# Two VectorE slots in score phases with three free banks when few PV matmuls are queued, and redrawn seeds

## Chip, cores, metric

One core of a Trainium2 chip. The metric is the device time of one execution in microseconds (us); medians of several runs are quoted.

## The reference, cut

Layer norm of `x` (2048 x 512, bf16), then multi-query attention with 32 heads of 16 and one shared K and V, times a gate from a two-layer SiLU network, plus the residual:

```python
xn = _layernorm(x)
s = _A_ref(xn, A_wq, A_wk, A_wv, A_wo)      # softmax(q k^T / 4) v, then wo; 32 heads, one K and V
g = _silu(_B_ref(xn, B_w1, B_w2))           # silu(silu(xn @ w1) @ w2), inner width 1792
return x + s * g
```

## The kernel before

The kernel contains a *planner*: a program that runs when the kernel is built, models the engines, and decides in what order every engine gets its instructions. The chip then follows that order, with semaphore waits where data need them. So a rule of the planner is no instruction; it changes only the order and the grouping.

What matters here:

- PE computes a *score phase*: three or four matmuls K x Q, each of 32 rows, into as many PSUM banks (`L860`, or `L859` in the changed file). One bank of scores is one *slot*.
- Each slot goes to ScalarE (an exact exp, `pa_sb`, then one PV matmul) or to VectorE (an approximation: one pass that writes bits, `db_sb`, and three shifted copies of these made by GpSimd integer adds, `ds_sb`, so four PV matmuls).
- Between phases PE works off *rounds* of four column-tiled matmuls: PV products from a queue (`L1228`, later `L1266`), or a *job*, a piece of the q, h, z or output projections (`L505`, later `L510`). A running job holds one of the seven banks.

How the planner splits the banks of a phase, before:

```python
n = len(banks)                     # banks free for this phase, at most 4
ab = act_need() - t                # how far ahead ScalarE is supplied
...
else:                              # three or four banks
    want = 2 if n == 4 or ab > a_low else 1      # slots for VectorE
...
want = min(want, 2 if bl < two else 1 if bl < one else 0)   # bl: VectorE's backlog
```

Thresholds such as `a_low`, `two`, `one` are shaken by seeded noise, and the seed is replaced every 64 phases:

```python
SEEDS, STRETCH, SPREAD = (1020, 3123, 1104, 3421, 7220, 2660, 1802, 97), 64, 0.1
def vary(x):
    return x * (1.0 + SPREAD * (rng[-1].random() - 0.5)) if rng else x
```

The softmax here doesn't subtract the row's maximum and nothing guards it: scores larger than these inputs give would overflow.

## Time and profile before

| | before |
|---|---|
| median of the runs | 672.18 us (672.05 to 672.34, 4 runs) |
| span of the profiled run | 670.41 us |
| start to first score phase | 11.04 us |
| floor of 632 cycles (worked out in the prediction) | 624.35 us |
| waits in these cycles | 9.40 us |
| nine other gaps (prologue) | 14.66 us |
| last score phase to end | 10.97 us |

The three parts of the middle and the two ends add up to the span (to 0.01 us). A *cycle* is the time from the start of one score phase to the start of the next, where only rounds lie between; its floor is what the steady beat of the trace gives (0.435 us for the phase, 0.2165 for each round; a count, not a measurement), and what exceeds the floor is called a wait. The profile's lines for this are shown in the prediction.

### The profile page before, as it was taken

The numbers are of one execution on the slowest core, as the hardware profiler recorded it, in microseconds if no ns is written. First come the engines' busy times: TensorE is split into PE (matmuls) and PEld (weight loads), VectorE is DVE, ScalarE is ACT, GpSimd is POOL, SyncE is SP. The second block draws the span as 40 slices with busy tenths as digits, with TensorE's granted clock in tenths as the row PEclk, the third lists the DMA queues.
The fourth block names the chain that finished last, engine by engine and source line by source line (L and its number), as shares of the span: only waits on it lengthen the run. The fifth ranks groups of instructions, "written<-read, shape, count | busy, mean of one in ns | idle before, by whom it ended". The sixth has DMA issues, their size and how long they took to land.

```text
span 670.4 us, 21190 instructions
## 1 busy us (share of the span) xinstructions
PE 658.4 (98%) x8958; PEld 191.4 (29%) x8958; DVE 608.6 (91%) x1085; ACT 651.5 (97%) x756; POOL 566.7 (85%) x564
## 2 busy tenths in 40 slices
PE   7999999999999999999999999999999999999997
PEld 4422222222222222222222222222222222222223
DVE  8989999999999999999899999998979999999963
ACT  6999999999999999999999999999999999999995
POOL 3049899998998889989899988898989998889993
PEclk9999999999999999999999999999999999999999
DMA  9500000000000000000000010000000000100000
GB/s 299 165 9 2 2 2 2 2 3 2 2 1 18 18 18 17 2 2 2 2 2 2 2 33 18 18 2 1 2 2 2 2 2 17 34 18 2 2 2 32
DMA packets 11821, 12.86 MB, mean 19 GB/s; under 512 B 1808, under 2 KB 11216, under 8 KB 11728
## 3 DMA queue, kind: packets, MB, share of 16 engines
q1 hardware_dynamic: 10928, 10.78, 5.0%
q8 instruction: 72, 1.18, 0.7%
q10 hardware_dynamic: 800, 0.72, 0.3%
q14 instruction: 21, 0.17, 0.1%
HBM read 8.95 MB, written 2.10 MB: 16 GB/s over the span
## 4 chain that ended last, share of the span: by engine, by line
PE 78%; ACT 12%; DVE 8%; issue 1%; DMA 0%; ACTq 0%; DVEq 0%
PE ps L1228 34%; PE ps L860 26%; PE ps L505 18%; ACT pa_sb L1572 11%; DVE db_sb L1090 3%; DVE stats_sb L452 1%; ACT t_sb L652 1%; DVE u_sb L654 1%; DMA ds_sb<-in_A_x_dram 0%; DVE xnT_sb L532 0%; DVE xn_sb L481 0%; DVE fin_sb L712 0%; DVE f_sb L1275 0%; DVE mv_sb L456 0%; DVE kt_sb L561 0%
## 5 line engine op out<-in xcount | busy, mean ns | idle before, releaser
L1157 POOL INT64_ADD ds_sb<-db_sb x552 | 561.0, 1038 | 87.5 <-DVE db_sb L1090 33.2
L1572 ACT ACTIVATE pa_sb<-ps 128x1024 bf16<-128x1024 f32 (+2 forms) x667 | 619.0, 1040 | 6.4 <-PE ps L860 3.5
L1090 DVE TENSOR_SCALAR db_sb<-ps 128x512 uint16<-128x512 f32 x736 | 474.4, 682 | 38.8 <-PE ps L860 27.5
L1228 PE MATMUL ps<-ds_sb,v_sb 128*32 128x512 bf16 x2208 | 265.9, 383 | 0.0
L860 PE MATMUL ps<-qt_sb,kt_sb 32*128 32x512 bf16 x2048 | 251.8, 385 | 4.4 <-ACT pa_sb L1572 1.1
L1228 PE MATMUL ps<-pa_sb,v_sb 128*32 128x512 bf16 x1312 | 242.4, 383 | 0.0
L1228 PE MATMUL ps<-db_sb,v_sb 128*32 128x512 bf16 x736 | 165.0, 384 | 0.3 <-DVE f_sb L1275 0.3
L860 PEld LDWEIGHTS ps<-qt_sb,kt_sb 32*128 32x128 bf16 x2048 | 63.1, 91 | 277.6 <-ACT pa_sb L1572 149.8
L1228 PEld LDWEIGHTS ps<-ds_sb,v_sb 128*32 128x32 bf16 x2208 | 65.6, 95 | 62.8 <-issue 46.1
L505 PE MATMUL ps<-xnT_sb,w_sb 128*32 128x512 bf16 x896 | 73.2, 384 | 0.0
L1228 PEld LDWEIGHTS ps<-pa_sb,v_sb 128*32 128x32 bf16 x1312 | 59.6, 95 | 36.5 <-issue 24.9
L505 PE MATMUL ps<-w_sb,u_sb 128*32 128x512 bf16 x816 | 64.2, 384 | 0.0
L1228 PEld LDWEIGHTS ps<-db_sb,v_sb 128*32 128x32 bf16 x736 | 40.9, 95 | 21.5 <-issue 14.5
L652 ACT ACTIVATE t_sb<-ps 128x512 bf16<-128x512 f32 x72 | 45.1, 627 | 0.0
L654 DVE SCALAR_TENSOR_TENSOR u_sb<-t_sb,ps 128x512 bf16<-128x512 bf16 x56 | 38.3, 683 | 1.3 <-ACT t_sb L652 0.3
L694 PE MATMUL ps<-w_sb,u_sb 32*128 32x512 bf16 x80 | 30.8, 385 | 0.0
L505 PEld LDWEIGHTS ps<-xnT_sb,w_sb 128*32 128x32 bf16 x896 | 17.5, 94 | 26.6 <-issue 20.6
L654 DVE SCALAR_TENSOR_TENSOR tmp_sb<-t_sb,ps 128x512 bf16<-128x512 bf16 x16 | 11.0, 688 | 12.3 <-ACT t_sb L652 12.2
L505 PEld LDWEIGHTS ps<-w_sb,u_sb 128*32 128x32 bf16 x816 | 15.6, 95 | 22.3 <-issue 18.5
L1275 DVE STREAM_TRANSPOSE f_sb<-ps 128x512 f32<-128x512 f32 x31 | 21.9, 707 | 0.1
L505 PE MATMUL ps<-wo_sb,on_sb 128*32 128x512 bf16 x256 | 19.2, 383 | 0.0
L505 PE MATMUL ps<-xnT_sb,wq_sb 128*32 128x512 bf16 x240 | 18.9, 384 | 0.0
(71 smaller groups left out, 161.9 us busy)
## 6 DMA issues: line engine op xcount, KB each, us to landing
w_sb<-in_B_w_dram SPq DMA_DIRECT2D x2, 1792.0 KB, 13.4
xr_sb<-in_A_x_dram SPq DMA_DIRECT2D x16, 128.0 KB, 2.3
out_dram<-ob_sb SPq DMA_DIRECT2D x16, 128.0 KB, 1.7
ds_sb<-in_A_x_dram SPq DMA_DIRECT2D x3, 512.0 KB, 6.9
wq_sb<-in_A_wq_dram SPq DMA_DIRECT2D x1, 512.0 KB, 5.1
wo_sb<-in_A_wo_dram SPq DMA_DIRECT2D x1, 512.0 KB, 16.0
kt_sb<-kt_sb ACTq DMA_DIRECT2D x4, 112.0 KB, 4.2
ds_sb<-in_A_x_dram ACTq DMA_DIRECT2D x2, 128.0 KB, 2.9
```

The lines of the kernel that those rows point to most:

```text
L452: ts_ = pl.add(Task(DV, 593.0, lambda v, t=t: v.bn_stats(stats_sb[:, t, :], x_tile(t)), [xkey(t)], [("st", t)], 1 + j, gate=(lambda j=j: S ...
L505: last = h.matmul(bank(b)[32 * j:32 * (j + 1), 0:n], lhsT=lhs(j), rhs=rhs, start=start, stop=stop, tile_position=(0, 32 * j), skip_group_c ...
L652: t1 = Task(AC, 490.0, lambda a: a.activation(t_sb[:, k, :], src, ACT.Tanh, scale=scale), [held], [("t", k)], 0, [t0])
L654: t2 = Task(DV, T_P, lambda v: v.scalar_tensor_tensor(out=dst, in0=t_sb[:, k, :], scalar=1.0, in1=src, op0=ALU.add, op1=ALU.mult), [held, ...
L694: return (lambda pe: pe.matmul(bank(b), lhsT=u_sb[rows, ft, r * P:(r + 1) * P], rhs=w2_sb[rows, ft, :], start=False, stop=last, tile_posit ...
L860: return pe.matmul(bank(b), lhsT=kt_sb[32 * i:32 * i + 32, g % 2, kt * P:(kt + 1) * P], rhs=qt_sb[32 * i:32 * i + 32, (g // 2) % NQR, :], ...
L1090: bt.P[i] = pl.add(Task(DV, T_P, lambda v, b=b, i=i, bb=bt.b: v.tensor_scalar(db_sb[:, bb, i * NQ:(i + 1) * NQ], bank(b), 128.0 * LOG2E, 1 ...
L1157: whole["po"].append(pl.add(Task(PO, T_P64, lambda g, cols=cols: g.int64_add(ds_sb[:, s, cols].bitcast(U64), db_sb[:, bt.b, cols].bitcast( ...
L1228: h = pe.matmul(bank(OB)[32 * i:32 * (i + 1), :], lhsT=lhs, rhs=rhs, start=s0, stop=s1, tile_position=(0, 32 * i), skip_group_check=True)
L1275: t1 = pl.add(Task(DV, T_TR, lambda v: v.transpose(f_sb[:, k, :], bank(OB)), [("ps", OB)], [("F", k)], 1, [norm.get(("m", g - 2))]))
L1572: op = pl.place(AC, 0.8333 * NQ * n + T_AF, lambda a: a.activation(pa_sb[:, s * NQ:(s + n) * NQ].rearrange("p (b n) -> p b n", n=NQ), ps3[ ...
```

## The change

The intent: a VectorE slot brings four PV matmuls, a ScalarE slot one. If PV work for the two open groups runs low, PE may go idle, so give VectorE more. The core of the diff:

```diff
-SEEDS, STRETCH, SPREAD = (1020, 3123, 1104, 3421, 7220, 2660, 1802, 97), 64, 0.1
-PIECE_MIN = 4
+SEEDS, STRETCH, SPREAD = (1020, 3123, 1104, 3421, 6268, 3265), 64, 0.2
+PIECE_MIN = {"z": 4, "h": 9, "q": 9, "w": 9}
...
+LATE, QUEUE = 0.0, 10
+Q3, Q4, J3, J4, N3, N4, SOLO = 10, -1, 1, 2, 1, 2, 0
...
-                want = 2 if n == 4 or ab > a_low else 1
...
+                queue = sum(len(q) for g in range(st["gO"], min(st["gO"] + 2, NG)) for q in pvq[g])
+                held = any(not a.fixed for a in active)
+                if held:
+                    want = J4 + (queue < vary(Q4)) if n == 4 else J3 + (queue < vary(Q3))
+                else:
+                    want = N4 if n == 4 else max(N3, 2 * (queue < vary(QUEUE)))
+                if ab > a_low:
+                    want = 2
```

Cut: a common helper that would let q, h and output jobs run row-tiled pieces (the limit of nine rounds is never reached), an extra slot in a bank that frees late, a filler for unfinished pieces (neither fires), switches that are off, and a condition on when the tail is made.

More of the change, by code (lines that the diff above doesn't have):

```diff
@@ L42 @@
 K = len(SHIFT)
+PH = []
 PE, AC, DV, PO, SP = "PE", "ACT", "DVE", "POOL", "SP"
@@ L65 @@
 EVAC = ()
-P3, AP3 = 0, 14
+LATE, QUEUE = 0.0, 10
+Q3, Q4, J3, J4, N3, N4, SOLO = 10, -1, 1, 2, 1, 2, 0
+END_DV = 0
+METER, RATE, R0 = (), 1.0, 1.0
 WIDE, NMIN, EARLY = 3, 3, 300.0
@@ L381, in bass_recurrent_scan__grouped_kv_mqa__dense_activation_silu__prompt_kernel @@
         outs = []
+        PH.clear()
         xv = xf.rearrange("(t p) d -> p t d", p=P)
@@ L497, in job @@
             jb.preds, jb.bank, jb.fixed, jb.mode, jb.gate = preds, bk, bk is not None, mode, gate
-            jb.pos, jb.end, jb.got, jb.left, jb.piece, jb.prev = 0, len(rounds), set(), len(rounds), None, None
+            jb.due, jb.pos, jb.end, jb.got, jb.left, jb.piece, jb.prev = None, 0, len(rounds), set(), len(rounds), None, None
             jb.tasks = {}
@@ L599, in xnT_ready, with product, rnd, mk @@
             return all(k in pl.lastw for k in xnT_keys(c))
+        def product(jb, lhs, rhs, needs):
+            n = len(jb.rounds)
+            def rnd(k):
+                def mk(b):
+                    last = jb.left == 1
+                    return lambda pe: col4(pe, b, lambda j: lhs(k, slice(0, P), 32 * j, 32), rhs(k, slice(0, P)), k == 0, last)
+                return mk
+            def piece(k, i, last):
+                rows, b = slice(32 * i, 32 * i + 32), jb.bank
+                return (lambda pe: pe.matmul(bank(b), lhsT=lhs(k, rows, 0, P), rhs=rhs(k, rows), start=False, stop=last,
+                                             tile_position=(32 * i, 0), skip_group_check=True), needs(k))
+            jb.rounds = [(rnd(k), needs(k), MM) for k in range(n)]
+            jb.piece = piece
         def mk_q(oi):
             c, o = divmod(oi, NOC)
-            def rnd(dc):
-                def mk(b):
-                    return lambda pe: col4(pe, b, lambda j: wq_sb[:, dc, P * o + 32 * j:P * o + 32 * (j + 1)],
-                                           xnT_sb[:, dc, c * NQ:(c + 1) * NQ], dc == 0, dc == NDC - 1)
-                return mk
             def consume(jb, op):
@@ L615, in consume @@
                 return [t]
-            job("q", oi, max(0.0, 2 * oi - Q_LEAD), [(rnd(dc), ["wq"] + xnT_keys(c), MM) for dc in range(NDC)],
-                consume,
-                gate=lambda: xnT_ready(c) and (oi < NQR or left_oct[oi - NQR] == 0))
+            jb = job("q", oi, max(0.0, 2 * oi - Q_LEAD), [None] * NDC, consume,
+                     gate=lambda: xnT_ready(c) and (oi < NQR or left_oct[oi - NQR] == 0))
+            product(jb, lambda k, rows, a, n: wq_sb[rows, k, P * o + a:P * o + a + n],
+                    lambda k, rows: xnT_sb[rows, k, c * NQ:(c + 1) * NQ], lambda k: ["wq"] + xnT_keys(c))
         def mk_q0(ta, tb, bk):
@@ L666, in mk_h @@
         def mk_h(c, ft, pace):
-            def rnd(dc):
-                def mk(b):
-                    return lambda pe: col4(pe, b, lambda j: w1_sb[:, dc, P * ft + 32 * j:P * ft + 32 * (j + 1)],
-                                           xnT_sb[:, dc, c * NQ:(c + 1) * NQ], dc == 0, dc == NDC - 1)
-                return mk
             def consume(jb, op):
@@ L678, in consume @@
                 return u_task[c, ft].first
-            job("h", (c, ft), pace, [(rnd(dc), ["w1"] + xnT_keys(c), MM) for dc in range(NDC)], consume)
+            jb = job("h", (c, ft), pace, [None] * NDC, consume)
+            product(jb, lambda k, rows, a, n: w1_sb[rows, k, P * ft + a:P * ft + a + n],
+                    lambda k, rows: xnT_sb[rows, k, c * NQ:(c + 1) * NQ], lambda k: ["w1"] + xnT_keys(c))
         def mk_z(tt, pace):
             c, r = divmod(tt, 4)
-            def rnd(ft):
-                def mk(b):
-                    last = jb.left == 1
-                    return lambda pe: col4(pe, b, lambda j: u_sb[:, ft, r * P + 32 * j:r * P + 32 * (j + 1)],
-                                           w2_sb[:, ft, :], ft == 0, last)
-                return mk
-            def piece(ft, i, last):
-                rows, b = slice(32 * i, 32 * i + 32), jb.bank
-                return (lambda pe: pe.matmul(bank(b), lhsT=u_sb[rows, ft, r * P:(r + 1) * P], rhs=w2_sb[rows, ft, :],
-                                             start=False, stop=last, tile_position=(32 * i, 0), skip_group_check=True),
-                        ["w2", ("u", ft)])
             def consume(jb, op):
@@ L703, in consume @@
                 return tmp_task[tt].first
-            jb = job("z", tt, pace, [(rnd(ft), ["w2", ("u", ft)], MM) for ft in range(NFT)], consume,
+            jb = job("z", tt, pace, [None] * NFT, consume,
                 gate=lambda: all((c, ft) in u_task and u_task[c, ft].op is not None for ft in range(NFT))
                 and (tt < 8 or tt - 8 in fin_task and fin_task[tt - 8].op is not None))
-            jb.piece = piece
+            product(jb, lambda k, rows, a, n: u_sb[rows, k, r * P + a:r * P + a + n],
+                    lambda k, rows: w2_sb[rows, k, :], lambda k: ["w2", ("u", k)])
         def scaled(tt, b):
@@ L736, in mk_w @@
             c, r = divmod(tt, 4)
-            def rnd(o):
-                def mk(b):
-                    return lambda pe: col4(pe, b, lambda j: on_sb[:, (NOC * c + o) % NON, r * P + 32 * j:r * P + 32 * (j + 1)],
-                                           wo_sb[:, o, :], o == 0, o == NOC - 1)
-                return mk
             def consume(jb, op):
@@ L749, in consume @@
                 return [t1]
-            job("w", tt, pace, [(rnd(o), ["wo", ("on", (NOC * c + o) % NON)], MM) for o in range(NOC)], consume,
-                gate=lambda: all(oi in t2_task and t2_task[oi].op is not None for oi in range(NOC * c, NOC * c + NOC))
+            jb = job("w", tt, pace, [None] * NOC, consume,
+                     gate=lambda: all(oi in t2_task and t2_task[oi].op is not None for oi in range(NOC * c, NOC * c + NOC))
                 and tmp_task.get(tt) is not None and tmp_task[tt].op is not None and tt in xr_task)
+            product(jb, lambda k, rows, a, n: on_sb[rows, (NOC * c + k) % NON, r * P + a:r * P + a + n],
+                    lambda k, rows: wo_sb[rows, k, :], lambda k: ["wo", ("on", (NOC * c + k) % NON)])
         mk_T([0], 0)
@@ L798, in bass_recurrent_scan__grouped_kv_mqa__dense_activation_silu__prompt_kernel @@
                 mk_w(sp[1], pace)
+        work = [jb for jb in jobs if jb.piece is not None and jb.kind in METER]
+        for j1, j2 in zip(work, work[1:]):
+            j1.due = j2.pace
         for tt in range(4):
@@ L970, in pe_start, with pick_d, pass_d, placed @@
             return max(t, last[-1].end + SWITCH)
+        def pick_d(avoid, t):
+            bt = d_batch()
+            if bt is None:
+                return None
+            need = [i for i in range(4) if i not in bt.slots and i not in avoid and left[bt.g, i] and slot_ok(bt.g, i)
+                    and slot_time(bt.g, i) <= t + 30]
+            if not need:
+                return None
+            i = max(need, key=lambda i: len(left[bt.g, i]))
+            avoid.add(i)
+            if not bt.slots:
+                batches.append(bt)
+                db_busy[bt.b] = 1
+            kt = take(bt.g, i)
+            bt.slots[i] = kt
+            return bt, bt.g, i, kt
+        def pass_d(b, bt, g, i, kt):
+            tot[g, i] += K
+            def placed(pop):
+                pool_free.append(b)
+                pvq[g][i].append((pop, v_lhs(1, g, kt), db_sb[:, bt.b, i * NQ:(i + 1) * NQ].bitcast(BF16),
+                                  [("Db", bt.b, i)] + v_reads(1, kt), ("d", bt)))
+            bt.P[i] = pl.add(Task(DV, T_P, lambda v: v.tensor_scalar(
+                db_sb[:, bt.b, i * NQ:(i + 1) * NQ], bank(b), 128.0 * LOG2E, 128.0 * (SHIFT_BETA + 127.0),
+                op0=ALU.mult, op1=ALU.add), [("ps", b)], [("Db", bt.b, i)], 0, on_place=placed))
         def do_S(t):
@@ L985, in do_S @@
             else:
-                want = 2 if n == 4 or ab > a_low else 1
-                tri = any(y - x == 2 for x, y in zip(sorted(banks), sorted(banks)[2:]))
-                if n == 4 and tri and (P3 == 1 or P3 == 2 and st.get("la", 2) == 2 or P3 == 3 and not [a for a in active if not a.fixed] or P3 == 4 and st.get("la", 2) == 2 and not [a for a in active if not a.fixed] or P3 == 5 and bl > 600 or P3 == 6 and a_pressure() >= AP3):
-                    want = 1
+                queue = sum(len(q) for g in range(st["gO"], min(st["gO"] + 2, NG)) for q in pvq[g])
[6 more added lines that the diff above has]
+                    want = 2
             pj = None
-            if n == 3 and pl.mode != "S":
+            late = [b for r, b in bank_times()[n:] if r <= t + LATE]
+            if bl > one or not want_d():
+                late = []
+            if n == 3 and pl.mode != "S" and not late:
                 for jb in active:
-                    if jb.piece is not None and jb.pos > 0 and (jb.got or jb.end - 1 - jb.pos >= PIECE_MIN):
+                    if jb.piece is not None and jb.pos > 0 and (jb.got or jb.end - 1 - jb.pos >= PIECE_MIN[jb.kind]):
                         pj = jb
@@ L999, in do_S @@
             while len(dslots) < want and want_d():
-                bt = d_batch()
-                if bt is None:
+                d = pick_d(avoid, t)
+                if d is None:
                     break
-                need = [i for i in range(4) if i not in bt.slots and i not in avoid and left[bt.g, i] and slot_ok(bt.g, i) and slot_time(bt.g, i) <= t + 30]
-                if not need:
-                    break
-                i = max(need, key=lambda i: len(left[bt.g, i]))
-                avoid.add(i)
-                if not bt.slots:
-                    batches.append(bt)
-                    db_busy[bt.b] = 1
-                kt = take(bt.g, i)
-                bt.slots[i] = kt
-                dslots.append((bt, bt.g, i, kt))
+                dslots.append(d)
             nd = len(dslots)
@@ L1034, in do_S @@
             abanks = best[1]
+            solo = False
+            if SOLO and len(sl) == 3:
+                pairs = [(x, y, z) for x in banks for y in banks for z in banks if z == y + 1 and x not in (y, z)]
+                if pairs:
+                    abanks, solo = min(pairs, key=lambda p: abs(p[0] - p[1])), True
             dbanks = [b for b in banks if b not in abanks]
@@ L1074, in do_S @@
             st["phases"] = st.get("phases", 0) + 1
+            PH.append((op.t0, any(not a.fixed for a in active), n, len(sl), nd, act_need() - op.t0 - MM, dve_backlog(), a_pressure(), sum(len(q) for g in range(st["gO"], min(st["gO"] + 2, NG)) for q in pvq[g])))
             if st["phases"] % STRETCH == 0 and len(SEEDS) > len(rng):
@@ L1078, in do_S @@
                 u = Unit()
-                u.slot, u.bank, u.vis = sl_, b, pl.vis(op, AC)
+                u.slot, u.bank, u.vis, u.solo = sl_, b, pl.vis(op, AC), solo and b == abanks[0]
                 units.append(u)
@@ L1082, in do_S @@
                 tot[g, i] += 1
-            for b, (bt, g, i, kt) in zip(dbanks, dslots):
-                tot[g, i] += K
-                def placed(pop, b=b, g=g, i=i, kt=kt, bt=bt):
-                    pool_free.append(b)
-                    pvq[g][i].append((pop, v_lhs(1, g, kt), db_sb[:, bt.b, i * NQ:(i + 1) * NQ].bitcast(BF16),
-                                      [("Db", bt.b, i)] + v_reads(1, kt), ("d", bt)))
-                bt.P[i] = pl.add(Task(DV, T_P, lambda v, b=b, i=i, bb=bt.b: v.tensor_scalar(
-                    db_sb[:, bb, i * NQ:(i + 1) * NQ], bank(b), 128.0 * LOG2E, 128.0 * (SHIFT_BETA + 127.0),
-                    op0=ALU.mult, op1=ALU.add), [("ps", b)], [("Db", bt.b, i)], 0, on_place=placed))
+            for b, d in zip(dbanks, dslots):
+                pass_d(b, *d)
+            late = [b for b in late if b in pool_free]
+            while late and len(seen) < 4 and len(dslots) < (2 if bl < two else 1) and want_d():
+                used = set(seen)
+                d = pick_d(used, t)
+                if d is None:
+                    break
+                b = late.pop(0)
+                _, g, i, kt = d
+                seen[i] = 1
+                t1 = max(op.t0 + 10.0, pl.ready(PE, s_reads(g, i, kt), [("ps", b)]))
+                pool_free.remove(b)
+                pl.place(PE, MM, lambda pe, b=b, g=g, i=i, kt=kt: s_mm(pe, b, g, i, kt), s_reads(g, i, kt), [("ps", b)], t0=t1)
+                pl.set_mode("S")
+                pass_d(b, *d)
+                dslots.append(d)
+                st["late"] = st.get("late", 0) + 1
             if dslots:
@@ L1153, in split @@
                 reads, ds_keys(s), lambda: URGENT if urgent() else 6, list(bt.P.values()),
-                on_place=placed_dv, ports=2, gate=lambda: URG_SPLIT and urgent() or len(shifts) >= DV_MIN))
+                on_place=placed_dv, ports=2, gate=lambda: len(shifts) >= DV_MIN or bt.g == NG - 1 and nleft[bt.g] < END_DV))
             for k in range(NPIECE):
@@ L1484, in do_fill, with metered @@
             st["fills"] = st.get("fills", 0) + 1
+        def metered(jb):
+            if jb.kind not in METER or jb.due is None or closing():
+                return False
+            n = len(jb.rounds)
+            return jb.pos > 0 and n - jb.left > (progress() - jb.pace) / max(1e-6, jb.due - jb.pace) * n * RATE + R0
         def pe_step():
@@ L1489, in pe_step @@
             start_jobs(t)
-            if st["assigned"] == NG * SLOTS and st["expn"] == len(units) and not tail["made"]:
+            if st["assigned"] == NG * SLOTS and st["expn"] == len(units) and not tail["made"] and all(
+                    tt in tmp_task for tt in range(NT - 4, NT)):
                 make_tail()
@@ L1499, in pe_step @@
                 col = ("pv", pr[1])
-            elif jr[0] == "go":
+            elif jr[0] == "go" and not (pr and pr[0] == "go" and metered(jr[1])):
                 col = ("job", jr[1])
@@ L1530, in pe_step @@
                 return True
+            for jb in active:
+                if ts is None and jb.got and jb.pos >= jb.end - 1:
+                    gap = min(i for i in range(4) if i not in jb.got)
+                    jb.got.add(gap)
+                    jb.left -= len(jb.got) == 4
+                    fn, rd = jb.piece(jb.end - 1, gap, jb.left == 0)
+                    jb.prev = pl.place(PE, MM, fn, sorted(set(rd), key=str), [("ps", jb.bank)],
+                                       t0=max(t, pe_start(pl.clk[PE], "S")), after=jb.prev)
+                    pl.set_mode("S")
+                    if len(jb.got) == 4:
+                        jb.got = set()
+                        jb.end -= 1
+                        finish(jb, jb.prev)
+                    return True
             nxt = INF
@@ L1554, in act_step @@
                     q.pop()
+                if q[0].solo:
+                    q = q[:1]
+                elif len(q) > 1 and any(u.solo for u in q):
+                    q = q[:[u.solo for u in q].index(True)]
                 n = len(q)
```

## The prediction

What some passages stand for in the profile before:

- *"0.22 us goes on the two changes"* (of tiling) is an estimate. From the start of the last round to that of the phase it is 0.321 us, from there to the start of the next round 0.321 (medians), where round follows round at 0.2165: 2 x 0.321 - 2 x 0.2165 = 0.21. It takes the phase's own matmuls as long as a round; the trace does not divide it further. They "go together": the four at 303.27 fill 0.39 us of the timeline, where one record is 0.385 long.
- *"594 x 0.42"*: for 0.42 us no weights are loaded before a phase even when nobody is late. 516 of 642 phases show just that (the brackets in the text), and the one at 659.44 shows it with no engine to wait for (`<-issue`).
- *"0.15 us each"* for three cycles of a single round: estimate, from no trace.

> **What bounds the kernel now.** I read the busy line of the page first, then the PE windows, then the PE timeline of a few steady microseconds, then the table of waits, and last the timeline of the tail.
>
> ```profile
> span 670.4 us, 21190 instructions
> PE 658.4 (98%) x8958; PEld 191.4 (29%) x8958; DVE 608.6 (91%) x1085; ACT 651.5 (97%) x756; POOL 566.7 (85%) x564
> ```
>
> Two engines look full, PE and ACT, so busy shares do not decide. The PE windows cut the span at the first and the last score phase (a score phase is one burst of L860 matmuls, K against Q, into three or four PSUM banks):
>
> ```profile
> 0.00:11.04 11.04, 8.43 (x129) 1.00 0.84 252
> 11.04:659.44 648.40, 642.81 (x8734) 1.00 0.05 15
> 659.44:670.40 10.96, 7.16 (x101) 1.00 0.14 49
> ```
>
> 97% of the span is one stream: score phase, some rounds of four column-tiled matmuls (PV, or one of the projections), score phase, and so on. The timeline shows its beat:
>
> ```profile
> 302.18 0.10 PEld L860 LDWEIGHTS ps<-qt_sb,kt_sb 32*128 32x128 bf16 x3 [0.42 <-ACT pa_sb L1572]
> ...
> 303.27 0.10 PEld L860 LDWEIGHTS ps<-qt_sb,kt_sb 32*128 32x128 bf16 x4 [0.42 <-DVE db_sb L1090]
> ...
> 304.14 0.10 PEld L860 LDWEIGHTS ps<-qt_sb,kt_sb 32*128 32x128 bf16 x3 [0.42 <-ACT pa_sb L1572]
> ...
> 305.06 0.10 PEld L860 LDWEIGHTS ps<-qt_sb,kt_sb 32*128 32x128 bf16 x3 [0.47 <-DVE db_sb L1090]
> ...
> 305.93 0.10 PEld L860 LDWEIGHTS ps<-qt_sb,kt_sb 32*128 32x128 bf16 x3 [0.42 <-ACT pa_sb L1572]
> ```
>
> From 302.18 to 303.27 twelve matmuls (three rounds) stand between two phases: 1.09 us. From 303.27 to 304.14 two rounds: 0.87 us. So a round costs about 0.2165 us, and a phase with both changes of tiling 0.435 us, whether it fills three banks or four. From 304.14 to 305.06 two rounds took 0.92: 0.05 us of real waiting. I sorted all PE starts of the trace in this way: 632 cycles have nothing but such rounds between two phases, 1614 rounds in all. 632 x 0.435 + 1614 x 0.2165 = 624.35 us; their measured sum is 633.75, so 9.4 us are waits. The nine other gaps, all in the prologue, hold 14.65 us. 624.35 + 9.4 + 14.65 = 648.4, the middle window. PE is the bound, and the whole of its waiting in the cycles is 9.4 us.
>
> The wait table seems to say something else:
>
> ```profile
> PEld ps L860 <- ACT pa_sb L1572: 149.8, 353, 0.7
> PEld ps L860 <- DVE db_sb L1090: 107.8, 241, 0.7
> ```
>
> These 594 waits sum to 257.6 us[...]. 594 x 0.42 = 249.5, which leaves about 8 us, in agreement with the 9.4.
>
> ACT is second:
>
> ```profile
> L1572 ACT ACTIVATE pa_sb<-ps 128x1024 bf16<-128x1024 f32 x637 | 603.2, 1052 | 5.3 <-PE ps L860 2.5 <-PE ps L694 0.7 <-DVE rstd_sb L472 0.4
> L1572 ACT ACTIVATE pa_sb<-ps 128x512 bf16<-128x512 f32 x26 | 17.0, 667 | 1.1 <-PE ps L860 1.1
> L1572 ACT ACTIVATE pa_sb<-ps 128x1536 bf16<-128x1536 f32 x4 | 5.6, 1451 | 0.0
> ```
>
> A record of two banks lasts 1052 ns, but starts follow each other at a median of 904 ns; one bank 477, three 1345, a tanh 477. 637 x 0.904 + 26 x 0.477 + 4 x 1.345 + 72 x 0.477 = 628 us of work in the 650 us between its first and last exp, so some 22 us of ACT's slack hide inside records counted as busy.
>
> [...] a phase costs 0.435 us where one round costs 0.2165, so about 0.22 us goes on the two changes, and its three or four matmuls go together. [...]
>
> **The change part by part.** A planning program in the kernel decides the order of instructions when it is built. I compared the two built programs, and let both builds write down their choices per phase (banks free, slots to ACT, slots to VectorE); no time is taken from the planner.
>
> (1) The named rule: with three free banks, two slots to VectorE if fewer than ten PV matmuls are queued. After the opening, the queue seen at a phase has a median near 35, and 11 to 12 at its first percentile in either kernel. In the changed build the rule gives two slots in ONE phase of 641, the 18th, with eight queued, at about 37.8 us by the old trace. So its direct worth is one redistribution early on.
>
> (2) Work. Every kind of instruction on PE, VectorE, GpSimd and the queues has the same count: 2048 score matmuls, 736 VectorE passes, 552 GpSimd adds, 80 row-tiled pieces.
>
> ```profile
> L1090 DVE TENSOR_SCALAR db_sb<-ps 128x512 uint16<-128x512 f32 x736 | 474.4, 682 | 38.8 <-PE ps L860 27.5 <-PE ps L694 8.1
> ```
>
> So VectorE's share does not rise at all. Only the grouping of exps differs: 624 of two banks (-13), 8 of three (+4), 40 of one (+14): -13 x 0.904 + 4 x 1.345 + 14 x 0.477 = +0.3 us on ACT, which has 22 us of slack: off the path.
>
> (3) The PE stream: 641 phases for 642, and 1614 rounds in cycles in both. One phase fewer: -0.43 us, on the path.
>
> (4) Switches in the text that do nothing: pieces for h, q and w need nine rounds left and those jobs have four; metering, solo exps and the VectorE end rule are off; the extra "late" slot and the new filler of unfinished pieces fired in no phase of this build.
>
> (5) Seeds and a doubled spread. From phase 18 on the plans differ. Waits by kind of cycle in the old trace: after two VectorE slots and three rounds, 38 cycles of mean 0.097 us (3.7); one VectorE slot, two rounds, then a four-bank phase, 52 of 0.043 (2.2); one VectorE slot, two rounds, then three banks, 274 of 0.006 (1.7); the rest 1.8. New counts 35, 57, 259: 3.4 + 2.4 + 1.6 + 1.8 = 9.2. Three cycles of a new kind have a single round after two VectorE slots; I put 0.15 us each on them as an estimate: +0.4. In sum 9.6 for 9.4, +0.2.
>
> (6) The tail.
>
> ```profile
> 659.44 0.09 PEld L860 LDWEIGHTS ps<-qt_sb,kt_sb 32*128 32x128 bf16 x2 [0.42 <-issue]
> ...
> 659.88 0.71 ACT L652 ACTIVATE t_sb<-ps 128x512 bf16<-128x512 f32 x1
> ...
> 660.37 1.14 ACT L1572 ACTIVATE pa_sb<-ps 128x1024 bf16<-128x1024 f32 x1
> ...
> 661.56 0.10 PEld L1228 LDWEIGHTS ps<-pa_sb,v_sb 128*32 128x32 bf16 x2 [0.17 <-ACT pa_sb L1572]
> ```
>
> Before, a tanh (0.49) stands between the last score phase and the last exp, and the last PV starts 2.12 us after that phase. In the changed order that tanh comes earlier, the last exps are single banks, and the last PV is some eight or nine rounds behind the phase: 0.32 + 8 x 0.2165 = 2.05, or 1.84 with seven. I take -0.2. The instructions from there to the last store are the same.
>
> Sum: -0.43 + 0.2 - 0.2 = -0.4 us. A re-drawn seed is normally kept because it came out better, so I lean 0.7 us further: 671.0 us.
>
> **Rivals.** (a) The rule as its words read: VectorE gets more slots, ScalarE is relieved, PE's queue never runs dry. For it: ACT at 97%. Against: the rule acts once, slots to VectorE stay 736, and PE, not ACT, sets the beat. Even if all 9.4 us of waits went, the time would be 662.7, 1.4% less: not 2%. (b) VectorE becomes the bound: two passes of 682 ns in a row free their banks late, and the waits after such phases (0.097 each) double. If it did so in all two-slot phases, +4 us, 676. Against: two-slot phases are 122 in both. (c) The new draw is simply a worse or better packing: 90 waits of over 40 ns make 8.7 us of the 9.4; as a scatter of independent events that is about sqrt(90) x 0.1 = 1 us either way: 670 to 672.
>
> **Range and chances.** The centre is 671.0; scatter of waits 1 us, tail 0.4, and the unknown lean 0.7 give about 1.3 us for one deviation, so 8 in 10 is 669.2 to 672.8. A gain of 2% needs 13.4 us, more than all the waits there are, with prologue order unchanged; a loss of 2% needs them to more than double. Faster 0.01, same 0.985, slower 0.005.
>
> **What would show it.** Right: PE beats of 0.87 and 1.09 us unchanged; 641 phases; waits in cycles 8 to 11 us; VectorE's 736 passes near 682 ns; ACT's two-bank starts at 904 ns; first 35 us equal to the old trace; last score phase 0 to 2 us earlier; 10.5 to 11 us after it. Wrong: a beat that changed with the mix of banks, a prologue that shifts, waits of L860 behind VectorE that grow by several us, or a granted clock below 1.00.

## The result

The changed kernel takes 670.80 us (670.55 to 670.98, 4 runs) against 672.18. The ratio is 0.9979, with a 95% interval of 0.9962 to 0.9996. It is "same" at 2%, and a small gain that the interval just separates from none.

The page of the changed kernel, span and busy times:

```profile
span 669.2 us, 21200 instructions
PE 657.5 (98%) x8957; PEld 190.4 (28%) x8958; DVE 609.8 (91%) x1085; ACT 650.7 (97%) x761; POOL 566.7 (85%) x564
```

Nothing moves here by more than 1.3 us, and the one thing that counts differently is ACT: 761 records for 756, the five additional exps. The PE windows of the changed kernel, cut at its own first and last score phase (stretch, PE busy, clock, DMA share, GB/s):

```profile
0.00:11.05 11.05, 8.22 (x127) 1.00 0.81 249
11.05:657.68 646.63, 641.82 (x8740) 1.00 0.05 15
657.68:669.20 11.52, 7.45 (x95) 1.00 0.14 48
```

The middle is 1.77 us shorter, the end some 0.5 us longer. The PE waits of the changed kernel (total us, times, longest):

```profile
PEld ps L859 <- ACT pa_sb L1635: 157.5, 371, 0.7
PEld ps L859 <- DVE db_sb L995: 100.6, 227, 0.8
```

That is 258.1 us in 598 waits, for 257.6 in 594 before. The totals hide the result: less the 0.42 us that each shows even when nobody is late, 7 us remain where 8 did. So I sorted the PE starts again, as for the prediction:

| us | first phase | floor | waits | prologue gaps | tail | span |
|---|---|---|---|---|---|---|
| before | 11.04 | 624.35 | 9.40 | 14.66 | 10.97 | 670.41 |
| after | 11.05 | 623.92 | 7.77 | 14.94 | 11.49 | 669.17 |
| difference | +0.01 | -0.43 | -1.63 | +0.28 | +0.52 | -1.24 |

The gain is in the waits. The +0.28 in the prologue belongs to this one profiled execution: two later kernels with the same plan up to there (e5 and e12 below) have 14.65 and 14.64.

**Which waits.** Most of the drop is in one kind of cycle: a four-bank phase with two VectorE slots while no job runs, then three rounds in which a job starts and takes a bank, then a three-bank phase. Two of the four lines of such a cycle in the timeline of the kernel before, the score phases at its two ends:

```profile
640.20 0.10 PEld L860 LDWEIGHTS ps<-qt_sb,kt_sb 32*128 32x128 bf16 x4 [0.48 <-DVE db_sb L1090]
...
641.40 0.10 PEld L860 LDWEIGHTS ps<-qt_sb,kt_sb 32*128 32x128 bf16 x3 [0.53 <-DVE db_sb L1090]
```

Three rounds should take 1.085 us; it took 1.20, and the bracket shows 0.53 instead of the 0.42 of a phase for which nobody is late: PE stood 0.11 us for a bank that a VectorE pass had not yet read out. I call these *late-job* cycles. There were 24 before (2.73 us) and there are 15 after (1.70 us): -1.03 of the -1.63. The other cycles of the same shape (four banks, three rounds, three banks) give another -0.62: 14 with 0.94 us before, 0.92 of it in seven that began with a job already running, and 20 with 0.32 us after. So this one shape has the whole drop, -1.65, and the changes in all other kinds cancel.

**The tail.** The last score phase starts 1.76 us earlier, but the end follows it 0.52 us later. In the timeline of the changed kernel, PE from its last score phase on, and the first VectorE transpose of the last normalisation:

```profile
657.67 0.10 PEld L859 LDWEIGHTS ps<-qt_sb,kt_sb 32*128 32x128 bf16 x2 [0.42 <-ACT pa_sb L1635]
...
658.53 0.10 PEld L1266 LDWEIGHTS ps<-pa_sb,v_sb 128*32 128x32 bf16 x2 [0.42 <-ACT pa_sb L1635]
...
659.02 0.09 PEld L1266 LDWEIGHTS ps<-pa_sb,v_sb 128*32 128x32 bf16 x1 [0.39 <-ACT pa_sb L1635]
...
659.51 0.09 PEld L1266 LDWEIGHTS ps<-pa_sb,v_sb 128*32 128x32 bf16 x1 [0.16 <-ACT pa_sb L1635]
...
660.00 0.09 PEld L1266 LDWEIGHTS ps<-pa_sb,v_sb 128*32 128x32 bf16 x1 [0.38 <-ACT pa_sb L1635]
...
660.65 0.45 DVE L1281 STREAM_TRANSPOSE f_sb<-ps 128x256 f32<-128x256 f32 x1 [6.53 <-PE ps L1266]
```

The PV rounds step at 0.49 us, close to the 0.477 between the starts of the last one-bank exps (658.33, 658.80, 659.28), not at 0.2165: PE follows ScalarE, exp by exp. The last PV that waits for an exp starts 2.33 us after the last phase (2.12 before), and the transpose 0.65 us after that (0.44 before).

### The profile page after: what moved, and what is told of

It is laid out like the page before. It is cut to its first block, busy times and chain, and to the rows that moved or that the text cites. A ratio compares the mean times of both kernels' runs of the same rounds, so it can differ in the third digit from the quotient of the medians.

```text
span 669.2 us, 21200 instructions
## 1 busy us (share of the span) xinstructions
PE 657.5 (98%) x8957; PEld 190.4 (28%) x8958; DVE 609.8 (91%) x1085; ACT 650.7 (97%) x761; POOL 566.7 (85%) x564
## 4 chain that ended last, share of the span: by engine, by line
PE 61%; ACT 30%; DVE 6%; DMA 1%; issue 1%; SPq 0%; POOL 0%; ACTq 0%; DVEq 0%
ACT pa_sb L1635 29%; PE ps L1266 26%; PE ps L859 20%; PE ps L510 14%; ACT t_sb L668 2%; DVE db_sb L995 2%; DVE stats_sb L457 1%; DMA ds_sb<-in_A_x_dram 1%; DVE u_sb L670 1%; DVE fin_sb L712 0%; DVE xn_sb L486 0%; DVE xnT_sb L537 0%; SPq L392 0%; POOL ds_sb L1195 0%; DVE f_sb L1313 0%
## 5 line engine op out<-in xcount | busy, mean ns | idle before, releaser
L1266 PE MATMUL ps<-ds_sb,v_sb 128*32 128x512 bf16 x2208 | 274.9, 383 | 0.0
L1266 PE MATMUL ps<-pa_sb,v_sb 128*32 128x512 bf16 x1312 | 245.0, 383 | 0.1
L1266 PE MATMUL ps<-db_sb,v_sb 128*32 128x512 bf16 x736 | 175.1, 383 | 0.0
L1266 PEld LDWEIGHTS ps<-ds_sb,v_sb 128*32 128x32 bf16 x2208 | 68.3, 95 | 60.3 <-issue 42.4
L1266 PEld LDWEIGHTS ps<-db_sb,v_sb 128*32 128x32 bf16 x736 | 43.2, 95 | 20.8 <-issue 16.3
L510 PEld LDWEIGHTS ps<-w_sb,u_sb 128*32 128x32 bf16 x816 | 14.9, 94 | 23.5 <-issue 20.8
```

The lines of the kernel that those rows point to most:

```text
L510: last = h.matmul(bank(b)[32 * j:32 * (j + 1), 0:n], lhsT=lhs(j), rhs=rhs, start=start, stop=stop, tile_position=(0, 32 * j), skip_group_c ...
L1266: h = pe.matmul(bank(OB)[32 * i:32 * (i + 1), :], lhsT=lhs, rhs=rhs, start=s0, stop=s1, tile_position=(0, 32 * i), skip_group_check=True)
```

## Experiments

Each is compared with the changed kernel's 670.8 us; the kernel before ran beside all of them at 672.1 to 672.2. The same sorting of PE starts (span of the profiled run, us; the last column is the number of late-job cycles and their waits):

| run | time | floor | waits | tail | span | late-job |
|---|---|---|---|---|---|---|
| before | 672.18 | 624.35 | 9.40 | 10.97 | 670.41 | 24, 2.73 |
| after | 670.80 | 623.92 | 7.77 | 11.49 | 669.17 | 15, 1.70 |
| e1_rule_off | 674.38 | 625.44 | 9.84 | 11.50 | 672.39 | 20, 2.25 |
| e2_rule_alone | 672.61 | 623.92 | 9.60 | 11.49 | 670.93 | 15, 1.76 |
| e3_old_draw | 671.43 | 625.00 | 8.15 | 10.83 | 669.62 | 15, 1.69 |
| e5_pe_more | 674.51 | 628.03 | 7.42 | 11.50 | 672.70 | 15, 1.68 |
| e6_act_more | 676.19 | 623.92 | 12.88 | 11.75 | 674.51 | 15, 1.70 |
| e9_drawA_off | 673.88 | 624.57 | 10.38 | 11.00 | 672.04 | 24, 2.69 |
| e12_dve_more | 672.76 | 623.92 | 9.95 | 11.49 | 670.96 | 15, 1.69 |

In the plans left out (e4, e7, e8, e10, e11) some neighbouring phases have no round between them, or a piece stands alone, so that floor and waits do not part as cleanly. In every plan listed a late-job cycle waits for 0.11 us; that reading holds. The rest of the waits has no such simple count.

The theory going in was A: the PE stream sets the time, through phases, rounds and late-job waits. The rivals were R: the rule is a gain by itself; S: the seeds are; D or P: any edit redraws the plan from there on, and the gain belongs to one picked draw.

### e1_rule_off: the changed kernel without the rule

```diff
-LATE, QUEUE = 0.0, 10
-Q3, Q4, ... = 10, ...
+LATE, QUEUE = 0.0, 0
+Q3, Q4, ... = 0, ...
```

> The changed kernel with the rule's threshold set to zero, same seeds, so three free banks never give two slots to VectorE on account of the queue. Only one phase (the 18th) is decided otherwise, but all after it is planned anew. Built program: 643 phases (changed kernel 641), 1683 rounds of four column-tiled matmuls (1678), 20 cycles of the late-job kind (15; see below). Theory A, the PE stream sets the time (0.435 us a phase, 0.2165 a round, 0.111 us of waiting in each cycle where a four-bank phase with two VectorE slots and no job is followed by three rounds and a three-bank phase with a job active): +0.87 +1.08 +0.56 = +2.5 us on 670.8, so 673.3. Theory R, the rule itself is the gain: back to the kernel before, 672.2, give or take 0.5. Theory N, the rule is worth nothing at all: 670.8.

Measured 674.38 us (674.21 to 674.61), 3.6 slower than with the rule and 2.2 slower than the kernel before. All three expectations were too low; A came nearest, but its count explains only part: the floor rose by 1.52, late-job waits by 0.55, and the other waits by 1.52 that nobody had foreseen. One decision, at the 18th phase, redraws the other 623 phases, and that is worth more than anything that the phase itself could save. Taken alone this run would seem to prove the rule; the next one does not.

### e2_rule_alone: the kernel before with the rule

```diff
-                want = 2 if n == 4 or ab > a_low else 1
+                queue = sum(len(q) for g in range(...two open groups...) for q in pvq[g])
+                want = 2 if n == 4 or ab > a_low or queue < 10 else 1
```

> The kernel before with the rule alone added (threshold ten, old seeds and spread). The rule acts in one phase. Built program: 641 phases for 642, 1676 rounds for 1677, 15 late-job cycles for 24, 732 VectorE slots for 736. Theory A: -0.43 -0.22 -1.0 = -1.65 us on 672.2, so 670.5. Theory R: the whole gain, 670.8. Theory S, the redrawn seeds are the gain: 672.2.

Measured 672.61 us (672.48 to 672.84), ratio to before 1.0005 (0.9992 to 1.0019): no gain. R falls in this form, and so does A as a sum of counts: the floor fell by the 0.43 counted and the late-job waits by 0.97, but the other waits rose by 1.17 and the tail by 0.52.

### e3_old_draw: the changed kernel with the old seeds and spread

```diff
-SEEDS, STRETCH, SPREAD = (1020, 3123, 1104, 3421, 6268, 3265), 64, 0.2
+SEEDS, STRETCH, SPREAD = (1020, 3123, 1104, 3421, 7220, 2660, 1802, 97), 64, 0.1
```

> The changed kernel with the old seeds and the old spread. Built program: 640 phases for 641, 1682 rounds for 1678, 15 late-job cycles for 15. Theory A: -0.43 +0.87 = +0.4, so 671.2. Theory R: 670.8. Theory S: 672.2.

Measured 671.43 us (671.36 to 671.50): between. With the old draw the rest of the change is worth 0.75 us over the kernel before, and the new draw adds 0.63. Neither S nor R alone has it. (The ratio to the kernel before is 0.9988, 0.9976 to 1.0001, so even the 0.75 is not quite clear of none; and since the changed code draws one more random number at the rule, the old seeds do not give the old noise number for number.) A was right on the sum here (671.2), not on its terms: against the changed kernel the floor rose by 1.08 and the waits by 0.38, and the tail fell by 0.66.

### e4_rule_30: the rule made to act often

```diff
-LATE, QUEUE = 0.0, 10
-Q3, Q4, ... = 10, ...
+LATE, QUEUE = 0.0, 30
+Q3, Q4, ... = 30, ...
```

> The changed kernel with the threshold at thirty queued matmuls instead of ten, so that the rule acts in 43 phases and not in one; 764 VectorE slots for 736, 638 phases, 1702 rounds, 24 late-job cycles. Theory R, more matmuls queued keep PE busy: faster than 670.8. Theory A: -1.3 +5.2 +1.0 = +4.9, so 675.7, or more if phases that follow a two-slot three-bank phase wait for their banks (two VectorE passes in a row last 1.2 us, a cycle of one round only 0.65): with 43 such waits of 0.2 us, 684.

Measured 686.02 us (685.88 to 686.20), 15.2 slower. The rule acts in 43 phases, VectorE gets 764 slots for 736, and PE has 28 x 3 = 84 more PV matmuls, 21 rounds or 4.5 us. Part of these rounds falls in the tail. The rest is waiting, which in this plan sums to about 21 us (7.8 in the changed kernel), ten short rounds of zeros that the planner put in as filler counted as waiting. Two lines of its profile, the busy line and ScalarE's waits for scores:

```profile
PE 664.5 (97%) x9082; PEld 196.0 (29%) x9082; DVE 620.2 (91%) x1113; ACT 649.1 (95%) x776; POOL 587.7 (86%) x585
...
ACT pa_sb L1635 <- PE ps L859: 14.9, 40, 1.1
```

ScalarE now stands 14.9 us for scores (3.2 in the changed kernel). So more queued PV matmuls did not keep PE busier here, they only took its time; what causes the rest of the waiting is not shown. The expectation's other branch, 684, came near in number but not in cause: the cycles behind the 43 phases wait for some 3 us in all, not for 43 x 0.2. (Its 1.2 us for two VectorE passes: in the profile before, passes in a row start 0.598 us apart, a median of 350 pairs, so two take 1.20.) R as its words read is refuted for this threshold: with the rule acting 43 times the kernel is slower, in the one plan tried.

### e5_pe_more, e6_act_more, e12_dve_more: what added work costs on each engine

Same plan as the changed kernel; work is added that the planner does not know of. PE: a round of zeros after each fiftieth PV round. ScalarE: a copy of 128 x 256 zeros after each thirtieth exp. VectorE: a transpose of 128 x 256 zeros after each thirty-third pass.

```diff
# e5, in do_pv's emit
+                if more:
+                    h = col4(pe, OB, lambda j: zer_sb[:, 32 * j:32 * (j + 1)], zer_sb[:, :], False, False)
# e6, behind the exp
+                    if more:
+                        h = a.activation(pad_sb[:, :], zer_sb[:, 0:256], ACT.Copy)
# e12, behind the VectorE pass
+                if more:
+                    h = v.transpose(pad_sb[:, :], zer_sb[:, 0:256])
```

> The changed kernel, same plan, with a round of four matmuls of zeros added behind every fiftieth full PV round: 19 rounds that the planner knows nothing of. Theory A, PE is the bound: 19 x 0.2165 = +4.1 us, so 674.9. If ScalarE were the bound and PE had slack: at most +1, 671.8.

> The changed kernel, same plan, with a copy of 256 zeros behind every thirtieth exp on ScalarE: 22 copies of some 0.3 us (an estimate: half a 512-column tanh of 0.477 plus a fixed part), 6.6 us of work that the planner knows nothing of. ScalarE as the bound: +6.6, so 677.4. Theory A, PE is the bound and ScalarE has some 20 us of slack in small pieces: each copy delays a bank by up to 0.3 us and PE loses only what its next phase then waits; +1 to +3, so 671.8 to 673.8.

> The changed kernel, same plan, with a transpose of 128 x 256 zeros behind every thirty-third VectorE pass: 22 of them, some 0.35 us each (half of the 0.707 us of a 512-column transpose in the old profile), 7.7 us of work that the planner knows nothing of. Theory A as it stood (VectorE has its own slack, 38 us idle ahead of its passes): +0 to +2 us on 670.8. Theory C, from what e6_act_more showed (5.4 of 6.75 us of added ScalarE work came through to the end, because each bank is freed just when PE wants it): the same share, 0.8, or +6.

| | added, us | time, us | came through |
|---|---|---|---|
| e5, 19 rounds on PE | 19 x 0.2165 = 4.1 | 674.51, +3.7 | 0.9 |
| e6, 22 copies on ACT | 22 x 0.307 = 6.75 | 676.19, +5.4; without the half-clock stretch 675.07, +4.3 | 0.6 |
| e12, 22 transposes on VectorE | 22 x 0.357 = 7.85 | 672.76, +2.0 | 0.25 |

The 0.307 and 0.357 are the steps from an added instruction's start to the next start on its engine. The "fixed part" in the expectation of e6 was an estimate; the starts in the profile before, 904 ns apart for 1024 columns and 477 for 512, give 2 x 477 - 904 = 50 ns for it. The answer on the added tile in e6 (its records, and those who waited for it: total us, times):

```profile
L1642 ACT ACTIVATE pad_sb<-zer_sb x22: 407/444/540, 37.6 to 655.1; 128x256 bf16<-128x256 bf16 x22
...
  PEld ps L860: 7.0, 13
```

and the same in e12:

```profile
L1003 DVE STREAM_TRANSPOSE pad_sb<-zer_sb x22: 426/435/440, 64.4 to 643.2; 128x256 bf16<-128x256 bf16 x22
...
  PEld ps L860: 4.1, 7
```

In e6, 13 of the 22 copies have a score phase of PE waiting directly behind them; in e12, 7 of the transposes have. So the reason given in the expectation of e12, that each bank is freed just when PE wants it, is shown for these 13 at most. Each such wait includes the usual 0.42; less that, 1.5 and 1.2 us stand directly behind, and the rest of the added waiting comes later. The plan is the same, so the floor, a count, is too; the waits grow by 5.11 and 2.18.

Not all of e6's 5.11 is the copies' doing. The same stretch of e6 and of the changed kernel (stretch, PE busy, clock, DMA share, GB/s):

```profile
39.09:42.51 3.42, 3.42 (x28) 0.50 0.00 0
39.09:42.51 3.42, 3.37 (x42) 1.00 0.00 0
```

For 3.4 us the granted clock was 0.50, and the two cycles in it took 1.87 and 1.83 us for 1.10 and 1.20 in the changed kernel: 1.4 us. Three of e6's four executions show 0.997 for the whole span, as this one does; the fourth, at 0.999, took 675.07. Whether the copy at 37.6 us brought the half clock on is not shown. Without it, (5.34 - 1.4) / 6.75 in the profile and 4.27 / 6.75 in the fourth execution give a share of about 0.6, not 0.8; so the share of 0.8 in the expectation of e12 above is too high.

So PE is on the path nearly all the time, as predicted. ScalarE, with 20-odd us of slack in sum, lets more than half of added work through, so that slack is for the most part not where a late bank could use it. VectorE lets a quarter through, at 91% busy, as theory A had it (+0 to +2) and not C.

### e7_no_late_job: late-job cycles taken away

```diff
+            st["wide"] = n == 4 and nd == 2
...
+                if not pro and st.get("wide") and not closing():
+                    return False        # in can_start
```

> The changed kernel, where a job may not start in the gap behind a four-bank phase with two VectorE slots. The late-job cycles fall from 15 to 8; 641 phases as before, 1679 rounds for 1678. Theory A with these waits alone counted: +0.2 -0.8 = -0.6, so 670.2. Rival P, any edit of the planner redraws all that follows and the other waits move by more than the class that was removed: the planner's own end (a model, which lay 3.6 to 4.8 us below the spans of six kernels run here) is 2.8 us later than for the changed kernel, so 673.4.

Measured 673.67 us (673.62 to 673.74), 2.9 slower, as rival P said. Eight late-job cycles are in the plan instead of fifteen, a matter of 0.8 us, and the redrawn plan loses over three elsewhere. So the late-job waits are a reading of where time went; taking them away by this edit did not gain.

### e8 to e11: the rule with other seeds

Two sets of ten fresh random seeds, not selected, each with the rule on (10) and off (0).

```diff
-SEEDS, STRETCH, SPREAD = (1020, 3123, 1104, 3421, 6268, 3265), 64, 0.2
+SEEDS, STRETCH, SPREAD = (5305, 2471, 6468, ...), 64, 0.2     # draw A; draw B: (8313, 3517, 614, ...)
```

> The changed kernel with ten fresh random seeds (5305 and on), spread and rule as in the change; the rule acts in two phases. Theory R, the rule is a gain whatever the seeds: 1 to 3 us below the same seeds with the rule off, which is run next. Theory D, the gain is that of one picked draw: the rule may win or lose with other seeds. Planner's end plus 5.9 us (its usual offset to the time here): 676.0.

> The fresh seeds of e8_drawA_on with the rule off. Theory R: 1 to 3 us slower than with it. Theory D: as likely faster; by the planner's end plus 5.9 us, 673.7, that is 2.3 us faster than with the rule.

> The changed kernel with another ten fresh random seeds (8313 and on); the rule acts in one phase. Theory R: 1 to 3 us below the same seeds with the rule off. Theory D: either way. Planner's end plus 5.9 us: 672.6.

> The fresh seeds of e10_drawB_on with the rule off. Theory R: 1 to 3 us slower than with it. Theory D: either way. Planner's end plus 5.9 us: 675.0, so here the rule would win by 2.4.

| seeds | rule on | rule off | on less off |
|---|---|---|---|
| those of the change | 670.80 | 674.38 (e1) | -3.6 |
| those of before, old code | 672.61 (e2) | 672.18 | +0.4 |
| draw A | 674.93 | 673.88 | +1.05 |
| draw B | 672.46 | 674.96 | -2.5 |

The sign changes from draw to draw: twice a gain, once a loss, once (e2) hardly a difference. Theory D fits: what the rule does to the time is set by the plan that it happens to lead to. For these four runs the forecast that held was the planner's own end plus 5.9 us: it was within 0.2 us in e9, e10 and e11, and 1.1 us too high in e8. Four pairs do not exclude a small mean gain of the rule; that stays open. The nine plans at this threshold or without the rule (before, after, e1, e2, e3, e8 to e11) have a mean of 673.1 us and a standard deviation of 1.5; the four unselected ones a mean of 674.1. The kernels before and after are both faster than all four unselected ones, as picked draws would be; that they were picked is likely.

These plans are not independent draws, though. In the traces the score phases of e1, e11 and e9, without the rule and with new seeds, follow each other as in the kernel before through phases 317, 335 and 482; those of e3 and e10, with the rule, as in the changed kernel through phase 415 (within 0.06 us a cycle, but for one cycle of the prologue that some executions have 0.3 us longer; e8 parts already at phase 69). So in these plans new seeds changed nothing in about the first half, and what parts the two groups there is the rule's one decision alone. It can be read: score matmul 1000, in phase 313 of each, starts at 330.12 to 330.19 us without the rule (before, e1, e11) and at 330.12 and 330.15 with it (e3, e10), with four rounds more done by then, at most 0.9 us of PE work. So all but some 0.9 us of the differences of -3.6 (e1) and -2.5 (draw B) arose later, where seeds and rule act together.

No version that was run beat 670.8.

## Why the prediction was right or wrong

**The total** was right: 671.0 predicted, 670.8 measured, in the range. The terms behind it were less good: their sum was -0.4 us, the profile shows -1.24, and the lean of -0.7 for a picked draw, a guess about how seeds are chosen and no mechanism, made up the rest. So that the total came within 0.2 us is in part luck: the waits fell by 1.83 us more than forecast, and the tail came out 0.72 us above its term. Two of the prediction's own signs were missed: waits of 8 to 11 us (7.77) and a tail of 10.5 to 11 us (11.49).

**The bound and the beat** were right. There is one phase fewer, -0.43 us, as predicted. The beat held in the cycles themselves: with two rounds a median of 0.870 us in both kernels, with three 1.086. And e5 shows that a round more costs 0.9 of its 0.2165 us in the end. The limit drawn from it, that 2% cannot be had from 9.4 us of waits, stood (672.18 - 9.4 is 662.8, not 662.7).

**"The rule acts once, so its direct worth is one redistribution"** was right as a count and incomplete as an argument. It left out that one decision redraws the rest, which was worth -3.6 to +1.05 us in four pairs. The seeds and the rule are not two parts whose effects add. And the plans differ from phase 18 on because of the rule, not of the seeds to which part (5) put it: without the rule (e1) the new seeds leave the plan as it was through phase 317.

**"Off the path" for ScalarE's additional 0.3 us** was wrong as reasoning. A slack found by adding up gaps was taken for slack at each moment; e6 shows that about 0.6 of added ScalarE work comes through. The term is small, so the sum hardly suffers.

**The term "9.6 for 9.4, +0.2" for the waits** failed most: it was -1.63. The step took a mean per kind of cycle, 0.097 us for "two VectorE slots, then three rounds", and multiplied it by the new count. That kind is a mix: before, 0.11 us where a job starts in the gap (24), 0.13 where one is already running (7), and 0.004 where there is none at the start or the end (7). The number of cycles fell from 38 to 35, but of those with a starting job from 24 to 15. Splitting by whether a job holds a bank, known from the build, would have given -1.0. The remaining -0.6 I could not have counted, and e1 and e2 show that such rests are of either sign.

**The tail, -0.2**, had the wrong sign: +0.52. The step counted PE rounds after the last phase. It saw that a tanh leaves the end of the chain, but not that the one-bank exps in its place start 0.477 us apart and that PE then waits for each.

**The rivals.** (a) fell with e4. (b) VectorE as the bound fell with e12, where only a quarter of the added VectorE work came through. (c), the draw, fits what happened; its scatter was put at 1 us, and nine plans, which share much, show 1.5.

## What to carry to other kernels

Where a planner or a scheduler is steered by thresholds and noise, any edit can redraw all that follows it: judge a rule by several draws with and without it, and count in the built program how often it acts before arguing about its worth. A slack that is a sum of gaps is not a slack at a given place; add a little work to one engine and see what share comes through (after a look at the test's own clock), for busy shares of 98, 97 and 91% here meant 0.9, about 0.6 and 0.25. And split the mean of a kind of wait by its cause before multiplying it by a new count.
